# Retention in half chunks on 64x64 quarters of TensorE, half blocks of 256 tokens, and three chunks ahead of the dense part

## The chip, the cores and the metric

The kernel runs on one core of a Trainium2 chip. The metric is device time in microseconds (us), median of several executions; lower is better. A profile is of one execution, and its span is about 2 us below that execution's time. In lines of profiles, PE is TensorE's products, PEld its weight loads, DVE VectorE, ACT ScalarE, POOL GpSimd and SP SyncE, which issues transfers; L257 is line 257 of the kernel. The clock of TensorE is told as the share of full speed that the profile says was granted.

## The reference

```python
# q, k, v: (4, 8, 768, 64); w_in: (512, 2048); w_out: (2048, 512)
gamma = 1.0 - 2.0 ** (-5.0 - np.arange(H))
for t in range(S):                       # retention, per batch and head
    state = gamma * state + outer(k[t], v[t])
    y[t] = scale * (q[t] @ state)
x = y as (3072, 512)                     # tokens x (heads * 64)
h = x @ w_in
out = (h - np.tanh(h)) @ w_out
```

The weights come as 64-bit floats, and the kernel turns each tile of them (16 of `w_in`, 16 of `w_out`) into float32 itself.

## The kernel before

Retention works in 24 chunks of 128 tokens, six in a batch. The decay is put into q and v by two multiplications on GpSimd. TensorE turns k and q (transposes them), makes the scores k'q, the state products k'v, and the outputs from the old state and from the masked scores. The dense part works in 96 steps: a step makes one tile of h (`up`), shrinks it on ScalarE and VectorE, and adds it into the outputs two steps later (`down`). Chunks are threaded between the steps.

```python
def convert(i):                      # one weight tile, from 64 bits to float32
    ...                              # two passes on ScalarE
    nc.vector.tensor_scalar(head..., HI_MIN, HI_MAX, op0=ALU.max, op1=ALU.min)
    nc.vector.tensor_scalar(head, head, 3, 0x3FFFFFF8, ...)
    nc.vector.scalar_tensor_tensor(head, in0=hi, scalar=0xC0000000, in1=head, ...)
    nc.vector.tensor_scalar(power, head, 0xFF800000, None, ...)
    nc.gpsimd.tensor_tensor(low, low, power.bitcast(F32), op=ALU.mult)
    nc.gpsimd.tensor_tensor(dst, low, head.bitcast(F32), op=ALU.add)

def scores(ci, tag):                 # two tiles: the contraction is 64 rows
    for h in range(H):
        r = ds(D * (h % 2), D)
        nc.tensor.matmul(sp[h % 2][:, ts(h // 2, P)], kT[r, h // 2], qT[r, h // 2], ...)
    ...                              # masks on VectorE

def outputs(ci, tag):
    ...                              # 8 products with the state, 128 tokens each
    if j < CPB - 1:                  # k'v; state = k'v + state before, on VectorE
        ...
    for h in range(H):               # with the masked scores
        i, p = h % 2, h // 2
        nc.tensor.matmul(yT[ds(D * i, D), ts(p, P)], vh[:, h], a[i][:, p], ...)

AHEAD = BLK + 1                      # five chunks before the first dense step
for ci in range(AHEAD):
    scores(ci, "h")
    if ci + 1 < AHEAD:
        turn(ci + 1)
    scale_chunk(ci + 2)              # GpSimd: q and v
    if ci:
        convert(ci - 1)
        load_weights(ci + 1)
    outputs(ci, "o")
    load_chunk(ci + 3)
...
for s, (n, m, first, last) in enumerate(steps):
    ci = with_chunk.get(s)
    if ci is not None:
        turn(ci)
    convert(AHEAD + s)
    load_weights(AHEAD + s + 2)
    up(n, m)                         # 4 products of 512 tokens
    ...                              # scores, scale_chunk, shrink, down, outputs
```

Of the kernel before, what the change touches and what calls it, by code (L numbers as in the profile page):

```python
# [15 lines left out]
P = 128  # L16
# [15 lines left out]
def kernel(  # L32
# [18 lines left out]

    nc = tc.nc
# [9 lines left out]
    BLK = 4  # L62
    NB = NCH // BLK
    TB = BLK * P
# [10 lines left out]
    op = ctx.enter_context(tc.tile_pool(name="op", bufs=2))  # L75
    ps = ctx.enter_context(tc.tile_pool(name="ps", bufs=1, space=bass.MemoryType.PSUM))
    ctx.enter_context(tc.manual_schedule())

    def bank(tag, name):

        return ps.tile([P, TB], F32, tag=tag, name=name, bufs={"o": 4, "h": 2, "t": 2}[tag])

    def quarters(t):
        return t.rearrange("p (n m) -> p n m", n=4)
# [9 lines left out]

    gq = columns(CPB * H)
    gv = columns(CPB * H)
    ident = columns(P)
    causal = columns(P)
# [5 lines left out]
    raws = {}  # L104

    def weight_ends(i):


        f, r = divmod(i, 2 * NC)
        if r < NC:  # L110
            return w1[:, r, ts(f, TB)], w_in[ts(r, P), ts(f, TB)]
        m = NC * f + r - NC
        return w2[:, m], w_out[ts(m, P)]

    NW = 2 * NM

    def load_weights(i):
        if i >= NW:
            return
        dst, src = weight_ends(i)  # L120
        if src.dtype == F32:
            nc.sync.dma_start(out=dst, in_=src)
            return
        raw = stage.tile([P, 2 * TB], U32, tag="raw", name=f"raw_{i}")
        nc.sync.dma_start(out=raw, in_=src.bitcast(U32))
        raws[i] = raw

    def convert(i):
# [10 lines left out]
        dst, _ = weight_ends(i)  # L139
        raw = raws.pop(i).rearrange("p (n two) -> p two n", two=2)  # L140
        lo, hi = raw[:, 0], raw[:, 1]
        head = stage.tile([P, TB], U32, tag="head", name=f"head_{i}")
        power = stage.tile([P, TB], U32, tag="power", name=f"power_{i}", bufs=1)
        low = stage.tile([P, TB], F32, tag="low", name=f"low_{i}")
# [10 lines left out]
        nc.gpsimd.tensor_tensor(dst, low, head.bitcast(F32), op=ALU.add)  # L155
# [4 lines left out]
    masked = {}  # L160
    xT = {}
    state = [None]
# [21 lines left out]
    def turn(ci):  # L184

        kh, qh, _ = loaded[ci]
        turned[ci] = []
        for nm, t in (("kT", kh), ("qT", qh)):
            tp = bank("t", f"{nm}p_{ci}")
            for p in range(NP):  # L190
                nc.tensor.transpose(tp[:, ts(p, P)],  # L191
                                    t[:, ds(2 * p, 2)].rearrange("p h d -> p (h d)"), ident)
            s = mid.tile([P, NP, P], F32, tag=nm, name=f"{nm}_{ci}")
            nc.scalar.copy(out=s, in_=quarters(tp))  # L194
            turned[ci].append(s)

    def scores(ci, tag):
        kT, qT = turned[ci]
        sp = [bank(tag, f"s{i}_{ci}") for i in range(2)]
        for h in range(H):  # L200
            r = ds(D * (h % 2), D)
            nc.tensor.matmul(sp[h % 2][:, ts(h // 2, P)], kT[r, h // 2], qT[r, h // 2],  # L202
                             start=True, stop=True)
        masked[ci] = []
        for i in range(2):
            a = mid.tile([P, NP, P], F32, tag=f"a{i}", name=f"a{i}_{ci}")
            nc.vector.tensor_tensor(a, quarters(sp[i]),  # L207
                                    causal[:, None, :].to_broadcast([P, NP, P]), op=ALU.mult)
            masked[ci].append(a)

    def outputs(ci, tag):
        j = ci % CPB
        n, nj = divmod(ci, BLK)
        if nj == 0:
            xT[n] = xp.tile([P, NP, TB], F32, tag="xT", name=f"xT_{n}")
        kh, _, vh = loaded.pop(ci)
        _, qT = turned.pop(ci)
        a = masked.pop(ci)
        before = state[0] if j else None
        yT = bank(tag, f"y_{ci}")  # L220
        if before is not None:
            for h in range(H):
                r = ds(D * (h % 2), D)
                nc.tensor.matmul(yT[r, ts(h // 2, P)], before[r, h // 2], qT[r, h // 2],  # L224
                                 start=(h // 2 == 0), stop=False, skip_group_check=True)
        if j < CPB - 1:
            kv = bank(tag, f"kv_{ci}").rearrange("p (n d) -> p n d", d=D)[:, :NP]
            for h in range(H):
                nc.tensor.matmul(kv[ds(D * (h % 2), D), h // 2], kh[:, h], vh[:, h],  # L229
                                 start=True, stop=True, skip_group_check=True)  # L230
            after = mid.tile([P, NP, D], F32, tag="state", name=f"state_{ci}")
            if before is None:
                nc.vector.tensor_copy(after, kv)
            else:
                nc.vector.tensor_tensor(after, kv, before, op=ALU.add)
            state[0] = after
        for h in range(H):
            i, p = h % 2, h // 2
            nc.tensor.matmul(yT[ds(D * i, D), ts(p, P)], vh[:, h], a[i][:, p],  # L239
                             start=(before is None and p == 0), stop=True,  # L240
                             skip_group_check=True)
        nc.scalar.copy(out=xT[n][:, :, ts(nj, P)], in_=quarters(yT))  # L242
# [4 lines left out]
    sums = {}  # L247

    def work(tag, bufs):
        return tmp.tile([P, TB], F32, tag=tag, name=tag, bufs=bufs)  # L250

    hps = {}

    def up(n, m):
        hp = bank("h", f"h_{n}_{m}")
        for c in range(NC):
            nc.tensor.matmul(hp, w1[:, c, ts(m, P)], xT[n][:, c], start=(c == 0),  # L257
                             stop=(c == NC - 1))
        hps[n, m] = hp

    def shrink(n, m):
        hp = hps.pop((n, m))
# [14 lines left out]
        g = gp.tile([P, TB], F32, tag="g", name=f"g_{n}_{m}")  # L277
        nc.vector.tensor_tensor(g, hp, u, op=ALU.mult)  # L278
        nc.vector.copy_predicated(g, large.bitcast(I32), th)  # L279
        gT[n, m] = g  # L280

    def down(n, m, j, first, last):

        if first:
            o_p[j] = bank("o", f"o_{n}_{m}_{j}")
        nc.tensor.matmul(o_p[j], gT[n, m][:, ts(j, P)], w2[:, m], start=first, stop=last)  # L286
        if not last:
            return
        done = m == NM - 1
        if j == 0 and n not in sums:  # L290
            sums[n] = [op.tile([P, BLK, DM], F32, tag="sum", name=f"sum_{n}"), set()]
        o, begun = sums[n][0][:, j], sums[n][1]
        if j in begun:
            nc.vector.tensor_tensor(o, o_p[j], o, op=ALU.add)
        elif j % 2:
            nc.vector.tensor_copy(o, o_p[j])
        else:
            nc.scalar.copy(out=o, in_=o_p[j])
        begun.add(j)
        if done:  # L300
            nc.sync.dma_start(out=out[ds(n * TB + j * P, P)], in_=o)
# [3 lines left out]
    Q = NM // 4  # L305
    runs = [[(0, 0)], [(1, 0), (1, 1)], [(0, 1), (0, 2)], [(1, 2), (1, 3)], [(0, 3)]]
    runs += [[(n, f) for f in range(4)] for n in range(2, NB)]
    steps = []
    for r in runs:
        tiles = [(n, Q * f + i) for n, f in r for i in range(Q)]  # L310
        steps += [(n, m, i == 0, i == len(tiles) - 1) for i, (n, m) in enumerate(tiles)]
# [3 lines left out]
    AHEAD = BLK + 1  # L315
    when = [0, 1, 2] + list(range(3, 27, 2)) + [28, 29, 30, 31]
    with_chunk = {s: AHEAD + i for i, s in enumerate(when)}

    for ci in range(2):
        load_chunk(ci)  # L320
    load_weights(0)
    load_chunk(2)
    load_weights(1)
    scale_chunk(0)
    turn(0)
    scale_chunk(1)
    for ci in range(AHEAD):
        scores(ci, "h")
        if ci + 1 < AHEAD:
            turn(ci + 1)  # L330
        scale_chunk(ci + 2)
        if ci:
            convert(ci - 1)
            load_weights(ci + 1)
        outputs(ci, "o")
        load_chunk(ci + 3)
    convert(AHEAD - 1)
    load_weights(AHEAD + 1)
    waiting = []

    def downs(lag):
        while len(waiting) > lag:
            n, m, first, last = waiting.pop(0)
            for j in range(BLK):
                down(n, m, j, first, last)

    for s, (n, m, first, last) in enumerate(steps):
        ci = with_chunk.get(s)
        if ci is not None:
            turn(ci)  # L350
        convert(AHEAD + s)
        load_weights(AHEAD + s + 2)
        up(n, m)
        if ci is not None:
            scores(ci, "t")
            scale_chunk(ci + 2)
        shrink(n, m)
        waiting.append((n, m, first, last))
        downs(LAG)
        if ci is not None:  # L360
            outputs(ci, "t")
            load_chunk(ci + 3)
    for j in range(BLK):
        for n, m, first, last in waiting:
            down(n, m, j, first, last)


def _tables(H, D, S=768):
# [12 lines left out]
            (t[None, :] >= t[:, None]).astype(np.float64),  # L381
# [38 lines left out]
```

## Time and profile before

| | before |
|---|---|
| time, median (range) | 806.59 us (805.2 to 807.6) |
| span of the profiled run | 803.4 us |
| TensorE busy, idle | 775.9 us, 27.5 us |
| VectorE busy | 516.1 us |
| two dense steps and one ordinary chunk | 18.60 us |

The prediction below quotes the lines of the page and of the chain that this rests on. They are read like this: TensorE is full from the fifth 20-us slice on, so what it does there is the time; before that the core waits, and what matters there is what TensorE waits for.

### The profile page before, as it was taken

What the parts mean: (1) busy time and instruction counts of PE and PEld (TensorE: products, weight loads), DVE (VectorE), ACT (ScalarE), POOL (GpSimd) and SP (SyncE); (2) the same over time, 40 slices, a digit from 0 to 9 for tenths busy, and PEclk for the clock granted to TensorE, in tenths of its full rate; (3) what the DMA queues carried; (4) which work ended last, traced back from release to release, by engine and by line L of the source; (5) the groups of instructions that cost most, each with busy time, mean ns of one, the idle gap of its engine ahead of it and who ended that gap; (6) DMA issues with size and microseconds to landing.
All of it is one profiled execution on the core that took longest, in us unless ns stands there. A gap on an engine that the chain in (4) does not pass through costs nothing.

```text
span 803.4 us, 8897 instructions
## 1 busy us (share of the span) xinstructions
PE 775.9 (97%) x3136; PEld 381.8 (48%) x3136; DVE 516.1 (64%) x796; ACT 364.5 (45%) x629; POOL 131.5 (16%) x116
## 2 busy tenths in 40 slices
PE   6769999999999999999999999999999999999997
PEld 5535555555555455544444444444444444444442
DVE  2876787777778765647655565555566666655553
ACT  3454554555555544334444444444444444444442
POOL 3763444333433341000000000000000000000000
PEclk9989999999999999999999999999999999999999
DMA  9875434244333322101000010000010000100001
GB/s 216 200 179 114 115 92 118 73 112 106 111 99 91 93 40 40 53 1 53 0 1 0 1 52 0 1 0 0 1 52 0 1 0 1 52 0 1 0 0 52
DMA packets 83131, 42.68 MB, mean 53 GB/s; under 512 B 75792, under 2 KB 75920, under 8 KB 83088
## 3 DMA queue, kind: packets, MB, share of 16 engines
q1 hardware_dynamic: 82944, 41.95, 20.4%
q8 instruction: 24, 0.39, 0.2%
q10 hardware_dynamic: 144, 0.18, 0.1%
q14 instruction: 19, 0.16, 0.1%
HBM read 35.83 MB, written 6.29 MB: 52 GB/s over the span
## 4 chain that ended last, share of the span: by engine, by line
PE 93%; DMA 2%; DVE 2%; ACT 1%; POOL 1%; issue 0%; SPq 0%; DVEq 0%; POOLq 0%; ACTq 0%
PE o L286 41%; PE h L257 41%; PE s L202 3%; PE y L239 2%; PE y L224 2%; PE qTp L191 1%; DMA q<-in_q_dram 1%; PE kv L229 1%; PE kTp L191 1%; DMA v<-in_v_dram 1%; ACT xT L242 0%; DVE head L149 0%; DVE head L151 0%; POOL q L180 0%; DVE a L207 0%
## 5 line engine op out<-in xcount | busy, mean ns | idle before, releaser
L257 PE MATMUL h<-xT,w 128*128 128x512 f32 x768 | 347.9, 595 | 5.6 <-POOL w L155 5.6
L286 PE MATMUL o<-w,g 128*128 128x512 f32 x768 | 347.0, 595 | 1.4 <-DVE g L279 1.4
L286 PEld LDWEIGHTS o<-w,g 128*128 128x128 f32 x768 | 144.4, 190 | 179.4 <-issue 174.3
L257 PEld LDWEIGHTS h<-xT,w 128*128 128x128 f32 x768 | 143.5, 190 | 176.5 <-issue 169.9
L265 ACT ACTIVATE u<-h 128x512 f32<-128x512 f32 x96 | 57.3, 597 | 311.6 <-PE h L257 311.6
L270 DVE TENSOR_TENSOR th<-h,th 128x512 f32<-128x512 f32 x96 | 66.2, 690 | 164.9 <-ACT th L266 164.9
L279 DVE COPY_PREDICATED g<-large,th 128x512 f32<-128x512 int32 x96 | 71.1, 740 | 10.2 <-ACT qT L194 0.5
L273 DVE SCALAR_TENSOR_TENSOR h<-q,h 128x512 f32<-128x512 f32 x96 | 66.8, 696 | 10.4 <-DVE h L271 0.5
L275 DVE SCALAR_TENSOR_TENSOR h<-q,h 128x512 f32<-128x512 f32 x96 | 66.8, 696 | 10.0
L278 DVE TENSOR_TENSOR g<-h,u 128x512 f32<-128x512 f32 x96 | 66.3, 691 | 7.1
L267 ACT ACTIVATE q<-u,tab 128x512 f32<-128x512 f32 x96 | 69.3, 722 | 0.0
L268 ACT ACTIVATE q<-u,tab 128x512 f32<-128x512 f32 x96 | 69.1, 720 | 0.0
L269 ACT ACTIVATE large<-u,tab 128x512 f32<-128x512 f32 x96 | 68.7, 716 | 0.0
L271 DVE SCALAR_TENSOR_TENSOR h<-u,h 128x512 f32<-128x512 f32 x96 | 65.8, 685 | 0.0
L154 POOL TENSOR_TENSOR low<-low,power 128x512 f32<-128x512 f32 x32 | 41.5, 1298 | 145.1 <-DVE power L153 145.1
L207 DVE TENSOR_TENSOR a<-s,tab 128x512 f32<-128x512 f32 x48 | 30.9, 684 | 48.6 <-PE s L202 48.6
L266 ACT ACTIVATE th<-h 128x512 f32<-128x512 f32 x96 | 56.8, 592 | 0.0
L242 ACT COPY xT<-y 128x512 f32<-128x512 f32 x24 | 14.1, 586 | 75.7 <-PE y L239 75.7
L155 POOL TENSOR_TENSOR w<-low,head 128x512 f32<-128x512 f32 x32 | 41.3, 1290 | 2.5
L202 PEld LDWEIGHTS s<-qT,kT 64*128 64x128 f32 x384 | 24.9, 199 | 16.9 <-issue 14.3
L180 POOL TENSOR_TENSOR q<-q,tab 128x512 f32<-128x512 f32 x24 | 25.0, 1043 | 37.6 <-DMA q<-in_q_dram 37.6
L202 PE MATMUL s<-qT,kT 64*128 64x128 f32 x384 | 29.7, 297 | 0.7 <-ACT qT L194 0.7
(29 smaller groups left out, 364.9 us busy)
## 6 DMA issues: line engine op xcount, KB each, us to landing
raw<-in_moe_w_in_dram SPq DMA_DIRECT2D x16, 512.0 KB, 4.1
raw<-in_moe_w_out_dram SPq DMA_DIRECT2D x16, 512.0 KB, 3.3
k<-in_k_dram SPq DMA_DIRECT2D x24, 256.0 KB, 4.1
q<-in_q_dram SPq DMA_DIRECT2D x24, 256.0 KB, 4.8
v<-in_v_dram SPq DMA_DIRECT2D x24, 256.0 KB, 4.5
out_dram<-sum SPq DMA_DIRECT2D x24, 256.0 KB, 2.1
tab<-in_tables_dram ACTq DMA_DIRECT2D x1, 177.5 KB, 3.0
```

Source lines behind the costliest of these rows:

```text
L202: nc.tensor.matmul(sp[h % 2][:, ts(h // 2, P)], kT[r, h // 2], qT[r, h // 2], start=True, stop=True)
L257: nc.tensor.matmul(hp, w1[:, c, ts(m, P)], xT[n][:, c], start=(c == 0), stop=(c == NC - 1))
L267: nc.scalar.activation(q0, u, AF.Square, bias=bias0)
L268: nc.scalar.activation(q1, u, AF.Square, bias=bias1, scale=math.sqrt(A))
L269: nc.scalar.activation(large, u, AF.Relu, bias=bias_m)
L270: nc.vector.tensor_tensor(th, hp, th, op=ALU.subtract)
L271: nc.vector.scalar_tensor_tensor(hp, in0=u, scalar=R, in1=hp, op0=ALU.subtract, op1=ALU.mult, reverse0=True)
L273: nc.vector.scalar_tensor_tensor(hp, in0=q0, scalar=C0, in1=hp, op0=ALU.add, op1=ALU.mult)
L275: nc.vector.scalar_tensor_tensor(hp, in0=q1, scalar=A * C1, in1=hp, op0=ALU.add, op1=ALU.mult)
L278: nc.vector.tensor_tensor(g, hp, u, op=ALU.mult)
L279: nc.vector.copy_predicated(g, large.bitcast(I32), th)
L286: nc.tensor.matmul(o_p[j], gT[n, m][:, ts(j, P)], w2[:, m], start=first, stop=last)
```

## The change

Its intent is to use all of TensorE's array in retention. A head has 64 columns. The profile of the kernel before lists the dense products as `128*128` and those of a head as `64*128` (scores), `128*64` (k'v and masked scores) and `64*64` (the old state): half or a quarter of the dense ones. The change cuts the chunks into halves of 64 tokens, which makes every retention product 64x64x64, and orders the products so that four neighbours lie on the four 64x64 quarters. To spread the outputs over both halves of columns, the two heads of odd pairs change places in y, and the rows of `w_in` are loaded in that order. Each group of four is now given two banks of PSUM (where the products of this kernel go), so blocks of the dense part shrink from 512 to 256 tokens, which frees two banks. Three chunks instead of five come before the first dense step. The start and the threading are written anew.

```diff
+    def products(ci):                       # next chunk's k'v and scores, on quarters
+        for p in range(NP):
+            for a in range(2):
+                for i in range(2):
+                    h, r = 2 * p + i, ds(D * a, D)
+                    nc.tensor.matmul(halves[ds(D * i, D), a, 1, p], kh[r, h], vh[r, h], ...)
+        ...                                 # 16 of scores likewise; mask; two states
+    def outputs(ci, meanwhile):
+        if j:
+            inter(0)                        # with the state, first half
+        inter(1)
+        intra(True)                         # masked scores, half of them
+        ...                                 # ScalarE reads `seen`; the rest waits for it
+        meanwhile()                         # a dense h product, or the next transposes
+        intra(False)
+        nc.scalar.copy(out=xT[n]..., in_=y)
+        products(ci + 1)
     def up(n, m2):
-        for c in range(NC):
-            nc.tensor.matmul(hp, w1[:, c, ts(m, P)], xT[n][:, c], ...)
+        for i in range(2):
+            for c in range(NC):             # 8 products of 256 tokens instead of 4 of 512
+                nc.tensor.matmul(hp[:, ts(i, TH)], w1[:, c, ts(2 * m2 + i, P)],
+                                 xT[n // 2][:, c, ts(n % 2, TH)], ...)
-    AHEAD = BLK + 1
+    AHEAD = 3
     for ci in range(AHEAD):
-        scores(ci, "h")
-        if ci + 1 < AHEAD:
-            turn(ci + 1)
         scale_chunk(ci + 2)
-        if ci:
-            convert(ci - 1)
-            load_weights(ci + 1)
-        outputs(ci, "o")
+        outputs(ci, lambda: turn(ci + 2, "h"))
         load_chunk(ci + 3)
+        turn_copy(ci + 2)
+        convert(ci)
+        load_weights(ci + 3)
     for s, (n, m2, first, last) in enumerate(steps):
+        for i in with_weights.get(s, []):   # {0: [3, 4], 1: [5, 6], 2: [7], ...}
+            convert(i)
+            load_weights(i + 3)
         ...
-            outputs(ci, "t")
+            scale_chunk(ci + 2)
+            outputs(ci, lambda: up(n, m2))
+            load_chunk(ci + 3)
         shrink(n, m2)
         ...
+            turn(ci + 2)
+            turn_copy(ci + 2)
```

Unconverted weights have three buffers instead of two.

## The prediction

> **What bounds the kernel now.** I read the first parts of the page, then the chain that ended last, then that chain in order of time.
>
> ```profile
> PE 775.9 (97%) x3136; PEld 381.8 (48%) x3136; DVE 516.1 (64%) x796; ACT 364.5 (45%) x629; POOL 131.5 (16%) x116
> PE   6769999999999999999999999999999999999997
> DMA  9875434244333322101000010000010000100001
> PE 93%; DMA 2%; DVE 2%; ACT 1%; POOL 1%; issue 0%; SPq 0%; DVEq 0%; POOLq 0%; ACTq 0%
> L257 PE MATMUL h<-xT,w 128*128 128x512 f32 x768 | 347.9, 595 | 5.6 <-POOL w L155 5.6
> L286 PE MATMUL o<-w,g 128*128 128x512 f32 x768 | 347.0, 595 | 1.4 <-DVE g L279 1.4
> ```
>
> TensorE is the chain from about 80 us on; only the first four slices (80 us) have gaps, and there DMA is at its fullest. TensorE idles 803.4-775.9 = 27.5 us in all. Two kinds of work fill it: the two dense products, and the retention that is threaded between them. The chain in order of time shows one against the other:
>
> ```profile
> 142.10 3.63 PE h L257 x8
> 145.73 3.43 PE o L286 x8
> 149.16 0.44 PE kTp L191 x4
> 149.60 0.44 PE qTp L191 x4
> 150.04 3.44 PE h L257 x8
> 153.47 1.09 PE s L202 x16
> 154.56 3.63 PE o L286 x8
> 158.19 0.62 PE kv L229 x16
> 158.81 0.88 PE y L239 x16
> 159.69 3.63 PE h L257 x8
> ...
> 175.78 1.02 PE y L224 x16
> 176.80 0.62 PE kv L229 x16
> 177.42 0.88 PE y L239 x16
> 178.29 3.63 PE h L257 x8
> ```
>
> Eight 512-column instructions take 3.43, so one is 0.429 us; a dense step (8 h, 8 o) is 6.87. From 159.69 to 178.29 is 18.60 us: two steps (13.74) and one chunk, so an ordinary chunk costs 4.87. From 142.10 to 159.69 is 17.59, so the first chunk of a batch, without the state product at L224, costs 3.85. The same reading of the h at 123.96 and at 142.10 gives 4.40 for the last chunk of a batch, which has no kv. All 96 steps are 659 us; 24 chunks are 16x4.87+4x3.85+4x4.40 = 111 us; the remaining 33 us are the start (28) and the tail (5 to 6).
>
> [...] An h or o group after a retention group takes 3.63, not 3.43: 0.20 for the switch into the full array. A full-array transpose of 128 columns takes 0.44/4 = 0.110; the 16 instructions of y at L239, also 128 columns, take 0.88, so 0.055 each: two tiles run at the price of one. L224 (0.14 above 8x0.110) and kv (0.18 above 8x0.055) show the switch into a tiled mode, about 0.16. [...] The trace has only pairs, at 29 to 55 ns an instruction[...]. [...] here every written product appears as two instructions (768 for 384)[...].
>
> **The change, part by part.**
>
> Retention on quarters. A chunk's 8+8+8+8 products become 16 of scores, 16 of kv, 16 with the state and 16 within the half chunks: 128 instructions of 64 columns on 64x64 quarters. In banks and rows they are laid out so that four may run at once (odd pairs' heads swapped, and a wait on ScalarE between the two inner halves with the dense h product put in between). By halves of the 128-column time, a group of four takes about 0.056: 32 groups are 1.79. Transposes stay at 0.88. Switches are two into quarters and two back: 2x0.16+2x0.20 = 0.72. Sum 3.39. I take 3.45 for a little slack in supplying 256 instructions and weight loads; 3.22 for a batch's first chunk (4 groups fewer); the last chunk no longer saves kv.
>
> Half blocks. The h products become 1536 instructions of 256 columns. From 0.110 at 128 and 0.429 at 512 columns there are about 2.7 ns fixed in each, so 768 more cost 2.1 us. Weight loads stay hidden: a 128-column load fits under a 0.110 us transpose now, and will lie under 0.216. The number of steps, the o products, and the tanh work on ScalarE and VectorE stay the same.
>
> VectorE and ScalarE. Masks fall from 48 to 24 at 0.684 (-16 us), states rise from 20 to 44 at 0.41 (+10), sums gain 6 adds (+4). ScalarE's transposed copies are half as many and twice as long, and there are 48 tiny reads. None of it is on the path in steady state: in 17.2 us VectorE has 8.4 of tanh work, about 5 of weight conversion, 0.7 of mask, 0.8 of states, some 15 in all.
>
> The start. Fewer chunks come before the first h (three instead of five), but the order inside changes. In the new order on GpSimd the conversion of weight tile 0 stands ahead of the scaling of chunk 3, and on VectorE behind the mask and states of chunk 1. So each early chunk is a circle: second inner half, products (1.1), mask and states (1.5), four VectorE conversions (2.0 when GpSimd is quiet), two GpSimd ones (2.6), scaling of q (1.04), transposes (0.7), second inner half (0.5): 9.5 us. The old kernel's chunks, which were paced by DMA, came every 5 to 6. Taking the landing of chunk 2's q at 16.8 (14.6 before, plus half a MB more ahead of it at about 0.24 MB/us), the second inner half of chunks 1 and 2 ends at 29 and 39. Three conversions then stand before chunk 5's scaling, so its transposes end at 54, those of chunk 6 at 65, and of chunk 7 at 75.5, when TensorE itself (10.3 us a step with a chunk) is the pace. At 85.8, 4 h groups, 2 o groups and chunks 0 to 6 would be done. The kernel before, at 86.74, has the same 4 and 2 and chunks 0 to 8. The two chunks owed are 6.9, less 2.7 already done of them (products of 7, transposes of 7 and 8): 4.2. Against the 0.9 that the clock is ahead, the start loses 3.3 us. This is my least certain step.
>
> **The sum.** After that point the kernel before has chunks 9 to 23: ten at 4.87, three at 4.40, two at 3.85, 69.6 in all. In the new one they are 13x3.45+2x3.22 = 51.3, so 18.3 saved. 803.4-18.3+2.1+3.3 = 790.5 of span. The timed median lies 3.2 above the profiled span (806.59 against 803.4), so 793.7. I go to 792 because my count of the start has few overlaps in it.
>
> **Rivals.** (1) Quarters run only in pairs. [...] if only the neighbour overlaps, a chunk costs 1.79 more, 5.2, and the 15 chunks lose about 9 us instead of saving 18: about 818. For it: no group of four in this trace. Against: four pairs at L239 already hide one head completely behind the other. One chance in eight. [...] (2) The start is bound by transfers alone, not by the conversion circle. Some 13 MB by the end of step 4 at 0.21 MB/us (0 to 20 us: 216 GB/s) is 65 us against the 96 my circle gives; a start half way there makes 780. For it: DMA is at nine tenths in the first slices. Against: the critical chain of the kernel before already goes through head and w conversions at 29 to 50 us, and one h product waits 5.6 us for w. (3) A new wait in steady state: ScalarE's reads that let the second inner half begin stand behind a conversion, and the scaling of q behind VectorE's tanh work with only some 2 us to spare before its transposes. A wait of 1 us in each of 12 chunk steps would make 804. (4) The weight loads of the 256-column products come into the open: against it, the transposes above.
>
> **Range and chances.** Full fours with a good start reach 776; fours spoilt by supply, or a microsecond of wait per chunk, reach 808. The line of 2% is at 790.5, just under my middle: faster 0.43, within 2% 0.51, slower 0.06.
>
> **What would show it.** Right: in the chain, a 16-product group (32 instructions) of kv or scores takes 0.45 to 0.6 us, h groups are 16 instructions in 3.45 (+0.2 after a switch), two steps with a chunk take 17.2 to 17.5, TensorE's gaps lie below 75 us and name GpSimd's scaled q or w. Wrong: 32 instructions in 0.9 us (pairs), repeated TensorE waits for ScalarE's small reads, for q, or for states beyond 100 us, or a first o group well before 65 us (the start was better than the circle).

Passages that told of hardware from outside this case are cut from the prediction, and the cuts are marked. None was a term of its sum, which came to 790.5 us of span and 793.7 us of time, put at 792. Under rival 1 a second case is cut (about 812 us, to which it gave one chance in eight); rival 1 begins again with "if only the neighbour overlaps". Some of the prediction's figures come without their place in the profile of the kernel before: 0.24 MB/us is the 244 GB/s there from 2 to 14 us; VectorE's 2.0 us are four instructions of 0.43, 0.43, 0.69 and 0.43 from 17.80 us on, with GpSimd idle; and for the 5 to 6 us of a chunk, the scalings of q that end GpSimd's waits for transfers begin at 9.68, 14.62, 20.88 and 26.68 us, 4.9, 6.3 and 5.8 apart.

## The result, and the profile after

| | before | after |
|---|---|---|
| time, median (range), same rounds | 806.77 us (805.2 to 807.6) | 797.58 us (797.43 to 798.99) |
| ratio | 1 | 0.9892 (0.9873 to 0.9911) |
| span of the profiled run | 803.4 us | 795.6 us |
| TensorE busy, idle | 775.9, 27.5 us | 760.5, 35.1 us |

A ratio is the mean time of one kernel's runs over that of the other's of the same rounds, so it is not quite the ratio of the medians. The change is 1.1% faster, inside the band of 2%. TensorE lost 15.4 us of work and gained 7.6 us of idleness.

From the page of the changed kernel: busy time, TensorE's slices and clock, the chain by engine, the h products (line, engine, operation, busy us, mean ns, idle before):

```profile
PE 760.5 (96%) x5504; PEld 515.9 (65%) x5504; DVE 508.4 (64%) x798; ACT 368.2 (46%) x660; POOL 131.0 (16%) x116
PE   4558999999999999999999999999999999999997
PEclk8577999999999999999999999999999999999999
PE 91%; DVE 3%; POOL 2%; SPq 1%; issue 1%; DMA 1%; ACT 1%; DVEq 0%; POOLq 0%; ACTq 0%
L342 PE MATMUL h<-xT,w 128*128 128x256 f32 x1536 | 351.9, 382 | 0.0
```

The first four slices are emptier than before (4, 5, 5, 8 tenths against 6, 7, 6, 9), and the clock is down in them, once to half. From the fifth slice on TensorE is full and at full clock.

The chain of the changed kernel in steady state (start us, us, what, instructions):

```profile
157.18 0.86 PE y L288 x48
158.04 3.65 PE h L342 x16
161.69 0.39 PE y L288 x16
162.08 0.47 PE s L243 x32
162.55 0.47 PE s L249 x32
163.01 3.63 PE o L374 x8
...
174.41 0.62 PE y L288 x32
```

Thirty-two retention instructions take 0.47 us, 14.6 ns each. Their single records start in fours, 6 to 7 ns apart within a four (161.902, 161.909, 161.915, 161.922) and 58 ns from one four to the next (161.902, 161.960, 162.019), which I read as four quarters at once. Two dense steps and one chunk last 174.41-157.18 = 17.23 us against 18.60, so an ordinary chunk costs 17.23-13.78 = 3.45 us instead of 4.87 (13.78 is two steps of 3.46+3.43). Between 120 and 330 us TensorE is busy without a gap.

**Where the time went.** I cut both runs where the h group of the seventh dense step begins, the chain of the kernel before first, then that of the changed one:

```profile
105.35 3.63 PE h L257 x8
```

```profile
115.84 3.46 PE h L342 x16
```

Both have six h groups behind them. The kernel before has finished chunks 0 to 9; the changed one has finished 0 to 8, made the products of 9, and turned k and q of 9 and 10. The changed kernel owes only the outputs of chunk 9 (about 1.5 us: its y groups take 0.86 and 0.39, and a dense group after them 3.65 instead of 3.46, the switch) and has 0.9 us of transposes in hand. From the cut to the end the kernel before needs 803.4-105.35 = 698.05 us, the changed one 795.6-115.84 = 679.76: 18.3 us saved. Up to the cut it is 10.5 us slower. So the change itself works in full, and more than half of what it earns is lost at the start.

The two longest of TensorE's waits in the changed kernel (total us, times, longest us):

```profile
PE kqTp L215 <- POOL q L200: 17.0, 6, 4.1
PE kqTp L215 <- DMA k<-in_k_dram: 9.0, 2, 4.7
```

Half of the 35.1 us idle is the turning of q, which waits for GpSimd to scale it (3.5 us of such waits before). One more wait is new, though short: 2.5 us for ScalarE's small read of `seen` in the first dense step, behind a conversion. GpSimd at the start of the changed kernel (start us, us, engine, line, operation; in brackets its idle time before, and what ended it):

```profile
18.23 1.04 POOL L200 TENSOR_TENSOR q<-q,tab 128x512 f32<-128x512 f32 x1 [6.22 <-DMA q<-in_q_dram]
...
26.47 1.26 POOL L171 TENSOR_TENSOR low<-low,power 128x512 f32<-128x512 f32 x1 [5.61 <-DVE power L170]
27.81 1.26 POOL L175 TENSOR_TENSOR w<-low,head 128x512 f32<-128x512 f32 x1
29.03 1.04 POOL L200 TENSOR_TENSOR q<-q,tab 128x512 f32<-128x512 f32 x1
...
37.35 1.26 POOL L171 TENSOR_TENSOR low<-low,power 128x512 f32<-128x512 f32 x1 [6.28 <-DVE power L170]
38.69 1.26 POOL L175 TENSOR_TENSOR w<-low,head 128x512 f32<-128x512 f32 x1
39.91 1.04 POOL L200 TENSOR_TENSOR q<-q,tab 128x512 f32<-128x512 f32 x1
```

GpSimd isn't busy: it stands still for 5.6 and 6.3 us, waiting for VectorE's part of a weight conversion, with the scaling of the next q behind it in its queue (chunk 3's starts here at 29.03 us, after the conversion, and at 24.06 in e1, where it stands ahead). VectorE in turn has that conversion behind the mask and the states of the current chunk, and TensorE cannot go on with the next chunk until q is scaled and turned. That is the circle of the prediction. It takes 39.91-29.03 = 10.9 us.

### The profile page after: what moved, and what is told of

Read it like the earlier page. It is cut to its first block, busy times and chain, and to the rows that moved or that the text cites. A ratio compares the mean times of both kernels' runs of the same rounds, so it can differ in the third digit from the quotient of the medians.

```text
span 795.6 us, 13784 instructions
## 1 busy us (share of the span) xinstructions
PE 760.5 (96%) x5504; PEld 515.9 (65%) x5504; DVE 508.4 (64%) x798; ACT 368.2 (46%) x660; POOL 131.0 (16%) x116
## 4 chain that ended last, share of the span: by engine, by line
PE 91%; DVE 3%; POOL 2%; SPq 1%; issue 1%; DMA 1%; ACT 1%; DVEq 0%; POOLq 0%; ACTq 0%
PE h L342 41%; PE o L374 41%; PE y L288 3%; PE kqTp L215 3%; PE s L249 1%; PE s L243 1%; POOL low L171 1%; SPq L191 1%; SPq L143 1%; DMA q<-in_q_dram 1%; POOL w L175 1%; POOL q L200 1%; DVE head L168 1%; DVE head L166 0%; DVE power L170 0%
## 5 line engine op out<-in xcount | busy, mean ns | idle before, releaser
L342 PE MATMUL h<-xT,w 128*128 128x256 f32 x1536 | 351.9, 382 | 0.0
L342 PEld LDWEIGHTS h<-xT,w 128*128 128x128 f32 x1536 | 291.1, 191 | 67.5 <-issue 30.4
L253 DVE TENSOR_TENSOR a<-s,tab 128x512 f32<-128x512 f32 x24 | 16.6, 692 | 77.5 <-PE s L249 77.5
L225 ACT COPY kqT<-kqTp 128x1024 f32<-128x1024 f32 (+1 forms) x27 | 24.5, 920 | 41.6 <-PE kqTp L215 41.6
L215 PE MATMUL kqTp<-tab,q 128*128 128x128 f32 x96 | 17.3, 310 | 17.0 <-POOL q L200 17.0
```

Source lines behind the costliest of these rows:

```text
L342: nc.tensor.matmul(hp[:, ts(i, TH)], w1[:, c, ts(2 * m2 + i, P)], xT[n // 2][:, c, ts(n % 2, TH)], start=(i == 0 and c == 0), stop=(c == N ...
```

## The experiments

In the table, "cut" is the start of the h group of the seventh step; "rest" is the span less the cut. All runs had 3 rounds, the last two 5.

| run | time us (range) | ratio to before | cut | rest |
|---|---|---|---|---|
| before | 806.77 | 1 | 105.35 | 698.05 |
| changed | 797.58 | 0.9892 | 115.84 | 679.8 |
| e1_scale_first | 791.19 (790.99 to 791.94) | 0.9808 | 109.74 | 679.8 |
| e2_cheap_convert | 773.42 (773.17 to 775.55) | 0.9595 | 91.57 | 679.8 |
| e3_keep_warm | 796.07 (795.33 to 796.24) | 0.9865 | 114.64 | 679.9 |
| e4_five_ahead | 803.31 (802.88 to 803.97) | 0.9958 | 122.37 | 679.8 |
| e5_convert_later | 795.10 (793.6 to 796.14) | 0.9855 | 109.48 | 683.9 |
| e6_same_quarter | 828.25 (827.19 to 829.27) | 1.0267 | 126.04 | 701.4 |
| e7_both | 796.78 (795.21 to 797.1) | 0.9878 | 108.15 | 685.2 |
| e8_both_raw4 | 787.88 (786.74 to 792.92) | 0.9779 | 101.54 | 685.5 |
| e9_early_steps_only | 780.37 (780.2 to 781.27) | 0.9678 | 99.70 | 679.8 |
| e10_and_warm | 781.84 (781.58 to 782.62) | 0.9697 | 100.57 | 679.8 |

The rest is 679.8 or 679.9 in every kernel that leaves the later order and the products alone. So a cut that comes earlier is a gain at the end, to a tenth of a microsecond, and start and rest can be judged apart. All results were correct except that of e2.

**e1: the coming chunk's scaling ahead of the conversion.** The theory is that the order on GpSimd makes the circle.

```diff
     turn_copy(1)
+    scale_chunk(2)
     for ci in range(AHEAD):
-        scale_chunk(ci + 2)
         outputs(ci, lambda: turn(ci + 2, "h"))
         load_chunk(ci + 3)
+        scale_chunk(ci + 3)
         turn_copy(ci + 2)
         convert(ci)
   # and in the steps: scale_chunk(ci + 3) behind load_chunk(ci + 3)
```

> One thing moved: the scaling of chunk n+3 on GpSimd stands ahead of the weight conversion of the same turn, not behind it. Circle theory (the late start of the changed kernel is the chain products, mask, conversion on VectorE, conversion on GpSimd, scaling of q, transposes): the q transposes of chunk 3 start near 25.5 us in place of 30.1, those of chunk 6 near 60 in place of 72.5, time 785 to 789 (changed kernel 797.6). Rival, DMA paces the start: the transposes move by under 2 us a chunk and the time stays above 793. Rival, the half clock alone: the same, above 793.

The time missed the expected 785 to 789: the cut came 6.1 us earlier, somewhat over half of the hoped gain. The q transposes of chunks 3 and 6 did come as foretold, at 25.16 and 60.64 us. The scaling of chunk 3's q began at 24.06 instead of 29.03, but chunk 4 could then not follow: its k waited 5.3 us for its transfer, which SyncE issues behind a load of weights that waits for a free buffer (in the chain, the load's issues end at 31.04 and k's begins at 31.14; over this run such loads of `w_in` wait 60.0 us for VectorE's L168, a reader of the buffer), and later states waited 2.6 and 5.9 us behind conversions on VectorE. The order is a cause, and behind it two others stand ready.

**e2: the first eight tiles converted by one ScalarE copy (wrong result).** It measures what the conversions cost the start.

```diff
         lo, hi = raw[:, 0], raw[:, 1]
+        if i < 8:
+            if isinstance(src, list):
+                hi = hi.rearrange("p (k n) -> p k n", k=2)
+            nc.scalar.activation(dst, hi.bitcast(F32), AF.Copy)
+            return
```

> Wrong result on purpose: weight tiles 0 to 7 are taken over by one ScalarE copy in place of two ScalarE, four VectorE and two GpSimd instructions; everything else and all transfers stay. Circle theory: the start loses its conversions, the chunks come at the pace of DMA (5 to 7 us in place of 10.9), time 780 to 786. Rival, DMA paces the start: 793 or more.

The start is 24.3 us shorter, more than I had expected (773.42 us lies below the 780 to 786), and nothing changes after the cut. So the conversions of the first eight tiles hold 24 us of the changed kernel's start on its path, far more than the 10.5 that it loses to the kernel before. It is a rough bound for what an order of them can earn (part of ScalarE's work went too), and no version to be used.

**e3: dummy products to keep the clock up.** The rival: what is slow in the circle is TensorE's half clock (0.50 granted from 20 to 40 us), supposed to come from its gaps.

```diff
+        for x, (t, tp) in enumerate(zip(loaded[ci], to)):
+            if x == 1 and 2 <= ci <= 6:
+                warm = bank("o", f"warm_{ci}")
+                for _ in range(14):
+                    nc.tensor.matmul(warm[:, :P], ident, ident, start=True, stop=True)
```

> 14 dummy products of 128 columns between the k and the q transposes of chunks 2 to 6, where TensorE waited 1 to 4 us at a granted clock of about a half. Clock theory (part of the late start is TensorE at half clock: about 1.5 us in each of five circles and 1 to 1.8 us in each of the first h groups): granted clock over 0.9 in 20 to 80 us, time 790 to 794. Rival (the wait on GpSimd hides the clock): within 2 us of 797.6, or worse if the dummies come into the way.

The clock of 20 to 40 us rose from 0.50 to 0.93 (0.83 and 0.91 in the next two slices), and the cut came 1.2 us earlier. The time is within the 2 us that the rival had named, not at the clock theory's 790 to 794. One circle did shrink, from 10.9 to 9.4 us (q transposes at 32.80 and 42.21), but the dummy products put off the first of them by 2.7 us (32.80 against 30.13), as they themselves were slow: the first 28 instructions took 5.25 us, 187 ns each, where the kernel before takes 110 ns for one of as many columns (0.44 us for four transposes). As the cause of the whole loss the clock falls; it is worth 1.5 us a circle, and dummy products don't bring it home.

**e4: five chunks ahead again.** What is the smaller number ahead worth?

```diff
-    AHEAD = 3
-    when = [0, 1, 2, 3, 4] + list(range(5, 28, 2)) + [28, 29, 30, 31]
+    AHEAD = 5
+    when = [0, 1, 2] + list(range(5, 28, 2)) + [28, 29, 30, 31]
-    with_weights = {0: [3, 4], 1: [5, 6], 2: [7]}
+    with_weights = {0: [5], 1: [6], 2: [7]}
```

> Changed kernel with five chunks ahead of the second part, as before, all else kept (quarters, half blocks, order of engines). If starting the second part at three chunks is worth what it intends, two h groups less by the time of chunk 6's transposes cost about 7 us: 803 to 806. Circle theory: the same number of conversions and scalings stands in the chain either way, with one conversion instead of three before chunk 5's scaling, so the transposes of chunk 6 come near 63 in place of 72.5 us and make up for the h groups: 794 to 800.

The cut came 6.5 us later, as the first of the two expectations had it; the 794 to 800 of the circle theory was a miss. The waits of q's transposes for GpSimd grow from 17.0 to 25.7 us: two more chunks go through the circle with no dense work beside them. So three ahead earns about 6 us of what the order loses.

**e5: conversions behind the outputs, in all steps.** If masks and states stand in the way of conversions, do the chunk first and convert later.

```diff
-        for i in with_weights.get(s, []):
-            convert(i)
-            load_weights(i + 3)
         ci = with_chunk.get(s)
         ...                              # up, or scale_chunk, outputs, load_chunk
+        for i in with_weights.get(s, []):
+            convert(i)
+            load_weights(i + 3)
         shrink(n, m2)
```

> Changed kernel, but in every step the weight conversions stand behind the chunk's retention and products (still ahead of the tanh work), so that masks, states, ScalarE's small reads and the scaling of q go first. Circle theory: the first three circles stay (q transposes of chunk 4 near 41 us), those of chunk 5 and 6 come 6 to 9 us earlier (59.8 and 72.5 before), the wait for the small reads in step 0 (2.5 us) goes: time 788 to 792. Rival (from then on DMA or VectorE paces): above 794.

A miss of 3 us, on the rival's side of 794, and an instructive one: the cut is 6.4 us earlier, but the rest is 4.1 us longer. TensorE waits 2.8 us there for sums on VectorE (e7 shows how).

**e6: four products of one quarter in a row.** The rivals to the reading of the steady state, both suppositions: if TensorE could look far ahead, the order of the quarters would not matter; if it took products strictly as they come, the quarters' gain in these groups would be gone.

```diff
-        for p in range(NP):
-            for a in range(2):
-                for i in range(2):
+        for a in range(2):
+            for i in range(2):
+                for p in range(NP):
   # for the k'v products and for the scores
```

> Changed kernel with the 16 kv and the 16 score products in another order only: four products of the same quarter, then the next quarter. The same work on the same quarters. If TensorE looks far enough ahead[...], a group of 32 instructions stays near 0.47 us and the time near 797.6. Rival, it looks only a few instructions ahead: quarters run one after the other, 32x0.055 = 1.76 us for a group, 1.29 more twice a chunk, 62 us in all over 24 chunks: 840 to 860.

In between. The chain of this run:

```profile
156.60 1.15 PE s L243 x29
157.74 0.06 PE s L249
157.80 0.00 PE s L243
157.80 0.06 PE s L249
157.86 0.00 PE s L243
157.86 0.05 PE s L249
157.91 0.00 PE s L243
157.92 1.15 PE s L249 x29
```

The 64 instructions of both groups take 159.07-156.60 = 2.47 us, 39 ns each against 14.6. The cycle of 17.23 us becomes 18.77, and 14 chunks after the cut by 1.54 are 21.6 us, just what the rest grew by (701.4-679.8). So with neighbours on different quarters the overlap was there, and with four products of one quarter in a row most of it was gone. The run also shows something that I had overlooked: in this chain, score instructions (L249) stand ahead of the last three of the 32 k'v instructions (L243 at 157.80, 157.86 and 157.91), though all k'v products stand before all scores in the program. The chain has the same for the next two chunks (L243 at 176.56, 176.62, 176.68 and at 195.10, 195.16, 195.21). By the order of the chain, then, score instructions went ahead of three k'v instructions here, and not of more. An estimate from this and from the 58 ns between the fours of the changed kernel: if one quarter's instructions are 58 ns apart, and every change of quarter overlaps by three of its eight instructions (four products of two) as this one does, the eight quarters of both groups take 8x5x58+3x58 ns = 2.49 us; measured are 2.47. The changed kernel's order asks for the same three, if a product's two instructions stand together: the fourth product's first has to pass the second ones of the three products before it.

**e7: e1 and e5 together.** No diff of its own: the edits of e1 and e5.

> The scaling first (as in e1) and the conversions later (as in e5) together. In e1 the saving stopped at TensorE waits of 2.6 and 5.9 us for states that stood behind conversions on VectorE. If that is so, these waits go and the two add up: 783 to 786. Rival: transfers that stand behind one another in the queue of SyncE (weight tile 3 waits for a conversion, chunk 4 stands behind it: 34.8 us in e1) pace it: 788 to 791.

A miss of more than 10 us, and outside the rival's 788 to 791 too. The cut came 7.7 us earlier, the rest grew by 5.4. TensorE's waits in this run:

```profile
PE kqTp L215 <- DMA k<-in_k_dram: 12.0, 3, 4.8
PE h L342 <- POOL w L175: 5.8, 1, 5.8
PE o L374 <- DVE sum L383: 4.1, 5, 1.4
```

Two new waits took the place of the old one. An h product waits for a weight tile whose conversion now comes too late. Between 120 and 330 us the only wait is the last of the three (4.1 of the 5.4 us; the remaining 1.3 us aren't listed as waits): an output bank isn't free until VectorE has added it up, and that addition now stands behind a conversion. So the order that helps the first steps harms the later ones.

**e8: e7 with four buffers for unconverted weights, their loads ahead of the conversion.** It takes away what chunk 4's transfers queue behind.

```diff
-            raw = stage.tile([P, 2 * BANK], U32, tag="raw", name=f"raw_{i}", bufs=3)
+            raw = stage.tile([P, 2 * BANK], U32, tag="raw", name=f"raw_{i}", bufs=4)
   # load_weights(i + 3) ahead of convert(i)
```

> e7 with a fourth buffer for raw weights, so that the loads of weight tiles stand ahead of the conversions that free a buffer and chunk 4's loads do not wait behind them. If the queue of SyncE is the next limit, chunk 4's k transposes come at 30 to 32 us in place of 34.8 and the time is 2 to 5 us under e7, 779 to 783. Rival: nothing under e7.

Chunk 4's k transposes came at 31.02 us, within the 30 to 32 foretold, and the run gained 8.9 us on e7 (2 to 5 expected). The 779 to 783 was missed all the same, since it was counted from the e7 that was hoped for. One execution took 792.92 us, the others at most 788.79. The cut came 14.3 us earlier than in the changed kernel, and 6.6 earlier than in e7. The rest stayed at 685.5, with the waits for sums.

**e9: the same, but conversions behind the outputs only in the first three steps.** It also converts tile 3 before the first step, so that step 0 has one conversion instead of two.

```diff
-    with_weights = {0: [3, 4], 1: [5, 6], 2: [7]}
+    EARLY = 3
+    with_weights = {0: [4], 1: [5], 2: [6, 7]}
   # e1's order of scaling; bufs=4, loads ahead of conversions;
   # load_weights(6) and convert(3) behind the first loop;
   # conversions behind the outputs where s < EARLY, at the old place elsewhere
```

> Scaling of the coming chunk ahead of the conversion everywhere, four buffers for unconverted weights, and conversions behind the outputs only in the first three steps, the changed kernel's order later. Theory (the start of 100 us is what the change loses, by a GpSimd and VectorE that do conversions and scalings in the wrong order, and the late sums behind conversions are what the run with both orders and four buffers gave back): that run started 14.3 us earlier and ended 9.7 earlier; without its late waits 779 to 783 us. Rival (the later waits come from the earlier start itself, as the weights arrive too late for it): 786 to 789 us, with new waits of TensorE for weights or sums between 120 and 260 us.

The rest is 679.8 again, and the cut is 16.1 us earlier than in the changed kernel, so the later waits came from the order and not from the earlier start. At 780.37 us, within the expected 779 to 783, it beats both kernels (0.9678). Five edits stand behind this number, and their shares weren't taken apart. GpSimd at its start:

```profile
24.16 1.04 POOL L200 TENSOR_TENSOR q<-q,tab 128x512 f32<-128x512 f32 x1 [2.93 <-DMA q<-in_q_dram]
...
28.00 1.28 POOL L171 TENSOR_TENSOR low<-low,power 128x512 f32<-128x512 f32 x1 [1.16 <-ACT kqT L225]
```

The scaling of q now begins when its transfer lands, and the conversion comes behind it. The DMA queues carry 207 and 186 GB/s between 20 and 60 us, against 142 and 135 in the two slices of the changed kernel: they are used more, where transfers had waited behind the circle.

**e10: e9 with six dummy products before q's transposes of chunks 2 to 4.** With short waits the clock might lie on the path.

> As the run with early steps only, with six dummy products before the turning of q of chunks 2 to 4, in time in which TensorE waits. Theory (the clock granted at the start matters little, as those waits end when GpSimd ends): within 2 us of that run. Rival (with the waits shorter, the half clock now lies on the path): 4 to 6 us below it.

The clock of 20 to 40 us rose from 0.67 to 0.92, and the run was 1.5 us slower than e9 (cut at 100.57). As expected, it stayed within 2 us of e9. Dummy products gained 1.5 us in the changed kernel's order and lost 1.5 in this one.

## Why the prediction was right

The time came out at 797.6, within the range and on the predicted side of the 2% line (within it had the largest chance, 0.51, hardly ahead of the 0.43 for faster). By its own steps:

**Quarters.** Right. The chain shows 3.45 us for an ordinary chunk, the predicted number. A group of 32 instructions takes 0.47 us, at the lower end of 0.45 to 0.6. Rival 1 (pairs, 0.9 us) falls, and e6 shows the condition for it (14.6 ns an instruction against 39).

**Half blocks.** Right: an h group takes 3.46 in place of 3.44 us, which over 96 groups is 1.9 us, near the 2.1 of the sum. (The two printed times of its working, 0.110 and 0.429 us, give 3.7 ns an instruction and not 2.7; measured are 0.02 us over eight more instructions, 2.5 ns.)

**The rest.** Worth 4 us more than predicted. With the prediction's terms, from the cut on, the kernel before has nine chunks at 4.87, three at 4.40 and two at 3.85, 64.7 us. The changed kernel has twelve at 3.45, two at 3.22 and 0.6 owed from chunks 9 and 10, 48.4 us, and 2.0 us for the shorter h instructions: 14.3 saved. The trace shows 18.3. Of the difference, 1.8 us are gaps of TensorE between 240 and 700 us of the kernel before (458.17 busy of 460.00; none in the changed one), and 1.4 the end, counted from the last h group's end: 16.1 us before, 14.7 after. In that end both kernels have 24 output instructions after the last h group, but 14 of them waited for the last tanh work before and 12 after (TensorE waits 1.4 us for it before, 0.5 after), in the two chains:

```profile
792.97 6.29 PE o L286 x14
```

```profile
786.52 5.43 PE o L374 x12
```

The prediction counted neither. Some 0.8 us stay unexplained.

**The start.** This is the step that the prediction called the least certain, and the term that was mis-sized: the mechanism was right and its size too small. It put the begin of the fifth step at 85.8 us; it was 95.16. At the cut that is a loss of 10.5 us in place of about 1. Where it went:

| end of | predicted | trace |
|---|---|---|
| second inner half of chunk 1 | 29 | 31.9 |
| second inner half of chunk 2 | 39 | 42.8 |
| transposes of chunk 5 | 54 | 60.9 |
| transposes of chunk 6 | 65 | 73.4 |
| transposes of chunk 7 | 75.5 | 85.1 |

The first 2.9 us are q of chunk 2, which landed at 18.2 instead of 16.8, and a circle of 10.9 instead of 9.5. In that circle TensorE runs at half clock (0.50 granted from 20 to 40 us): transposes 1.1 us instead of 0.7, products 1.8 (twice some 0.85 to 0.91) instead of 1.1, the inner half 0.64 instead of 0.5, together 1.2. The prediction counted full-clock durations for a TensorE that it had itself left mostly idle (from 20 to 40 us it is busy for 11.45 us at 0.50; in e3, with dummy products, for 16.36 at 0.93). Then three conversions stand ahead of chunk 5's scaling, and the prediction gave each of the two extra ones 2.75 us (54 less 39 less 9.5, halved), with VectorE's part (2.0) hidden or quiet. The trace gives each 3.95. VectorE there (start us, us):

```profile
46.39 0.43 DVE L166 TENSOR_SCALAR head<-head 128x512 uint32<-128x512 uint32 x1
46.85 0.69 DVE L168 SCALAR_TENSOR_TENSOR head<-raw,head 128x512 uint32<-128x512 uint32 x1
...
48.44 1.38 DVE L166 TENSOR_SCALAR head<-head 128x512 uint32<-128x512 uint32 x1
49.86 1.64 DVE L168 SCALAR_TENSOR_TENSOR head<-raw,head 128x512 uint32<-128x512 uint32 x1
```

The same instruction on the same shape takes 0.43 us alone and 1.38 when it meets GpSimd's multiplication of the tile before (48.22 to 49.54); the next takes 1.64 instead of 0.69 beside GpSimd's addition (49.62 to 50.95). It is so in the whole profile of the changed kernel: of the 32 instructions of L166 three run beside GpSimd and take 1.37 to 1.38 us, and the other 29 take 0.43; of L168 three take 1.64 to 1.65 and 29 take 0.69. In the lines above, each of the two ends 0.3 to 0.55 us after GpSimd's. So two conversions in a row run hardly side by side on the two engines: each costs 3.95 us, where VectorE's 2.0 and GpSimd's 2.6 in a row would be 4.6. This reading rests on the times in the trace; what makes the instructions longer it doesn't show, and no run took the overlap alone away. The last 2.7 us of the table, between the transposes of chunks 5 and 7, I have not put down to anything.

**Range and other rivals.** Rival 2 (transfers set the start, 780 us) falls for the changed kernel, since the DMA queues are little more than half busy from 20 to 60 us (0.59 and 0.50; they are full in the first 20 us, at 0.97, and its 13 MB at 0.21 are 62 us, not 65); it is what remains nearer at hand once the order is mended, as in e9 (0.86 and 0.81). Rival 3 (a new wait in steady state) did not show, though its small read cost 2.5 us once in the start; rival 4 (weight loads in the open) did not show either (16 h instructions of 256 columns, each with its load, take 3.46 us, against 3.44 for 8 of 512). But for 0.5 us at the end, the waits of TensorE lie below 75 us, and the largest sum names GpSimd's q, as foretold. The middle of 792 missed by 5.6 us. The span missed by 5.1 (795.6 against 790.5): the start took 9.4 more, the rest gave 4.0 back, and 0.3 are rounding. The distance from span to time was 2.0 instead of 3.2, as the profiled run of the kernel before (805.45 us) had been one of its faster ones. And I had gone 1.7 below the sum, for "few overlaps" in my count, when the overlaps cost time instead of saving it. That 9.4 us too little at the start became a miss of 5.6 is luck: the gaps and the end of the kernel before, which the prediction had not counted, gave back about 3 us of it. What the changed kernel could have been is e9: the quarters' 18 us stay, and the start is 5.6 us ahead of the old one instead of 10.5 behind.

## What to carry to other kernels

Where one engine's queue serves two streams, put ahead what the bounding engine waits for next, and behind it what has slack; and judge the first steps and the steady state apart, by a cut at the same work, because the order that helps one can harm the other (e5, e7 against e9). Small products on quarters of the array paid fully here where neighbours in program order lie on different quarters (14.6 ns an instruction against 39). A start that has been paced by one thing must be counted again when its order changes: with TensorE's clock as it is granted there (0.50 here), and with VectorE's times as they are beside GpSimd (1.38 us here in place of 0.43).
